# A diffusion transformer block on one core: V's order, the place of the half-head PV, the pieces of the last chunk, and the issue of the K weights

## The chip, the cores and the metric

The kernel runs on one core of a Trainium2 chip. The metric is device time in microseconds; lower is better.

Names: PE is TensorE's matmul, PEld its weight load, DVE VectorE, ACT ScalarE, POOL GpSimd, SP SyncE. "L688" is line 688 of that kernel's source; the change adds lines, so L1284 of the kernel before is L1289 of the changed one. "Half-head PV": a head has 576 columns, four times 128 plus 64; the two halves of 64 of both heads share one 128-row tile and are multiplied side by side in column tiles of 64.

## The reference

```python
B, N, D = 2, 256, 1152; F = 4 * D; H = 2; Dh = 576
mod = (silu(c) @ w_mod).reshape(B, 6, 1, D)     # shift_a, scale_a, gate_a, shift_m, scale_m, gate_m
h = layernorm(x) * (1 + scale_a) + shift_a
q, k, v = split(h @ wqkv)
a = softmax(q k^T * Dh**-0.5) v @ wo
x = x + gate_a * a
h2 = layernorm(x) * (1 + scale_m) + shift_m
return x + gate_m * (gelu(h2 @ w_fc1) @ w_fc2)
```

Everything is bfloat16 outside, with sums in float32.

## The kernel before

A scheduler inside the kernel fixes each engine's order at build time: PE and SP in program order, the others by a list scheduler with cost constants. The parts that matter here, with cuts (`...`):

```python
# start: loads on SP, in this order
for b in range(2):
    dma(X[:, 2 * b:2 * b + 2, :], xv[b], ..., "ld_x%d" % b)
for (ka, kb) in ((0, KC), (KC, KT)):
    for k0, k1 in ((0, 3), (3, 6), (6, 9)):
        dma(WSC[:, k0:k1, ka * P:kb * P], wmod_v[...], ..., "ld_sc%d_%d" % (ka, k0))   # scale weights
    for kt in range(ka, kb):
        dma(WK[:, kt, :], wqkv_v[:, kt, D:2 * D], ..., "ld_wk%d" % kt)                 # K weights
...
# middle: V pieces between softmaxes and transposes, then the modulation rows
v_proj(2, 0)
rows()            # gate rows: products in column tiles of 32, stored to DRAM, read back broadcast (GA)
...
v_proj(2, 1); v_proj(2, 2); v_proj(3, 0); rows_T(); v_proj(3, 1); v_proj(3, 2)
...
pv_halves()       # half-head PV: column tiles of 64, and its two evictions
for b in range(2):
    for h in range(2):
        pv(b, h)
wo_tile(0); wo_tile(1); wo_tile(2, ...)   # product with wo, times GA, plus x, layer norm
xn2_T(0)                                  # PE transposes the normalised tile 0
...
# end: the last token tile of fc2 in five pieces: 384, 384, 224, 96, 64 columns
```

## Time and profile before

| | kernel before |
|---|---|
| time, first three runs | 243.79, 243.87, 244.35 us |
| span of the profiled run | 242.3 us |
| PE busy | 238.4 us (98%) |
| first K product starts | 11.18 us |
| last data for the last store ready | 240.79 us |

How to read it: PE is busy all the time, so the end of the span is the sum of PE's own spacings, whatever starts PE's first dense work, and the tail after the last matmul. A line of a time line has start, duration, engine, source line, operation, shapes, count, and in brackets the engine's idle time before it with what ended it. The lines themselves stand in the prediction. One more is needed later, from the page's table of DMA queues (packets, MB, share of the engines):

```profile
q8 instruction: 14, 0.23, 0.4%
```

### The profile page before, as it was taken

To read this page: it belongs to the slowest core of one execution; us is meant where nothing else is said; L and a number is where in the kernel's file an instruction comes from. 1 tells how busy PE (TensorE), PEld (TensorE's weight loads), DVE (VectorE), ACT (ScalarE), POOL (GpSimd) and SP (SyncE) were. 2 spreads that over 40 slices of the span, in tenths; PEclk is the share of its full clock that TensorE was granted. 3 is DMA by queue.
4 is the path that set the end of the run, shared out by engine and by line. 5 is a ranking of instruction groups with operands and counts; after the bars stand their busy time and mean duration, and the time that the engine had idled before them with its cause. 6 is when DMAs were issued, how large, how long until landed. Compare 5 with 4: busy or idle time off the path is not lost.

```text
span 242.3 us, 4076 instructions
## 1 busy us (share of the span) xinstructions
PE 238.4 (98%) x1763; PEld 147.5 (61%) x1763; DVE 120.3 (50%) x218; ACT 67.0 (28%) x136; POOL 21.2 (9%) x39
## 2 busy tenths in 40 slices
PE   7999999999999999999999999999999999999996
PEld 2698854556667666898444444444566656656676
DVE  3814388696997699789999500000022222111112
ACT  5820350355424107973233322222000000000000
POOL 1400000000021186400000000020000000000000
PEclk9999999999999999999999999999999999999999
DMA  6999999999996999989953498012000000000001
GB/s 241 330 381 392 391 392 391 397 413 405 391 356 196 351 395 391 391 266 394 314 164 82 150 320 313 0 29 72 0 16 19 16 16 19 16 16 16 19 24 27
DMA packets 30140, 51.59 MB, mean 213 GB/s; under 512 B 1703, under 2 KB 15787, under 8 KB 30123
## 3 DMA queue, kind: packets, MB, share of 16 engines
q1 hardware_dynamic: 29680, 50.14, 58.0%
q0 software_dynamic: 416, 1.19, 1.6%
q8 instruction: 14, 0.23, 0.4%
q14 instruction: 3, 0.02, 0.0%
q10 hardware_dynamic: 27, 0.00, 0.0%
HBM read 50.14 MB, written 1.19 MB: 212 GB/s over the span
## 4 chain that ended last, share of the span: by engine, by line
PE 97%; DVE 2%; POOL 0%; issue 0%; ACT 0%; DVEq 0%; POOLq 0%
PE psum L688 95%; PE psum L691 2%; DVE arena L739 1%; DVE arena L760 0%; POOL arena L711 0%; DVE arena L740 0%; DVE arena L1284 0%; DVE arena L1285 0%; POOL arena L710 0%; ACT arena L726 0%; DVE arena L727 0%; DVE arena L732 0%; DVE arena L742 0%; POOL arena L717 0%; POOL arena L715 0%
## 5 line engine op out<-in xcount | busy, mean ns | idle before, releaser
L688 PE MATMUL psum<-arena 128*128 128x384 bf16 (+10 forms) x1674 | 234.9, 306 | 1.6 <-POOL arena L711 1.5
L688 PEld LDWEIGHTS psum<-arena 128*128 128x128 bf16 (+3 forms) x1674 | 142.3, 97 | 90.0 <-issue 3.8
L1079 DVE SCALAR_TENSOR_TENSOR arena<-arena 128x1152 f32<-128x1152 bf16 x32 | 44.7, 1414 | 0.6
L1284 DVE TENSOR_TENSOR arena<-psum,arena 128x384 f32<-128x384 f32 (+3 forms) x14 | 7.0, 501 | 68.0 <-PE psum L688 68.0
L1193 ACT ACTIVATE arena<-psum 128x512 bf16<-128x512 f32 (+1 forms) x44 | 22.4, 520 | 42.7 <-PE psum L688 42.7
L683 ACT ACTIVATE arena<-psum 128x512 bf16<-128x512 f32 (+6 forms) x37 | 19.6, 549 | 39.5 <-PE psum L688 37.1
L685 DVE CAST arena<-psum 128x512 bf16<-128x512 f32 (+3 forms) x13 | 8.2, 641 | 11.4 <-PE psum L688 11.3
L669 POOL DMA_DIRECT2D dit_scratch<-arena x3 | 1.8, 616 | 115.7 <-DVE arena L685 58.9
L1161 POOL TENSOR_TENSOR arena<-arena 128x384 f32<-128x384 f32 x12 | 10.9, 910 | 10.8 <-DVE arena L1160 9.5
L1106 DVE CAST arena<-psum 72x32 bf16<-72x32 f32 x1 | 0.2, 186 | 21.3 <-PE psum L688 21.3
L739 DVE BATCH_NORM_STATS2 arena<-arena 128x6 f32<-128x384 f32 (+1 forms) x18 | 9.5, 552 | 0.1
L1166 ACT ACTIVATE arena<-arena 128x1152 bf16<-128x1152 f32 x4 | 5.3, 1345 | 11.9 <-DVE arena L1165 11.9
L691 PEld LDWEIGHTS psum<-arena 128*128 128x128 bf16 (+1 forms) x89 | 5.8, 98 | 2.5 <-issue 0.8
L1160 DVE TENSOR_TENSOR arena<-psum,arena 128x384 f32<-128x384 f32 x12 | 6.5, 549 | 1.6 <-DMA arena<-dit_scratch 1.6
L1285 DVE TENSOR_TENSOR arena<-arena 128x384 bf16<-128x384 f32 (+3 forms) x14 | 7.0, 501 | 0.5
L691 PE MATMUL psum<-arena 128*128 128x128 bf16 (+1 forms) x89 | 7.1, 219 | 0.1
L1180 DVE TENSOR_SCALAR arena<-psum,arena 128x128 bf16<-128x128 bf16 x20 | 5.4, 341 | 1.9 <-PE psum L691 1.9
L1183 ACT ACTIVATE arena<-psum,arena 128x128 bf16<-128x128 bf16 x16 | 6.0, 456 | 0.9 <-PE psum L688 0.6
L1086 DVE TENSOR_REDUCE arena<-arena 128x36 f32<-128x1152 f32 x4 | 5.4, 1348 | 0.0
L1083 DVE STREAM_TRANSPOSE arena<-arena 128x1152 f32<-128x1152 f32 x4 | 5.4, 1364 | 0.0
L1009 ACT ACTIVATE arena<-psum,arena 128x256 bf16<-128x256 f32 x8 | 3.7, 472 | 1.3 <-PE psum L688 0.9
L743 POOL TENSOR_TENSOR arena<-arena 128x1 f32<-128x1 f32 x6 | 3.6, 596 | 2.0 <-DVE arena L742 2.0
(48 smaller groups left out, 44.9 us busy)
## 6 DMA issues: line engine op xcount, KB each, us to landing
arena<-in_w_fc_dram SPq DMA_DIRECT2D x9, 1152.0 KB, 7.3
arena<-in_w_fc_dram SPq DMA_DIRECT2D x4, 2592.0 KB, 17.2
arena<-in_wqkv_dram SPq DMA_DIRECT2D x18, 288.0 KB, 10.2
arena<-in_w_mod_dram SPq DMA_DIRECT2D x3, 1728.0 KB, 20.2
arena<-in_w_mod_dram SPq DMA_DIRECT2D x3, 864.0 KB, 13.7
arena<-in_w_mod_dram SPq DMA_DIRECT2D x9, 288.0 KB, 10.5
arena<-in_wqkv_dram SPq DMA_DIRECT2D x1, 2592.0 KB, 16.6
arena<-in_wo_dram SPq DMA_DIRECT2D x1, 2592.0 KB, 24.4
```

What stands on the lines that cost most here:

```text
L683: act(c_act(n), lambda e: e.activation(out=dst, in_=src, func=ACTF.Copy), [src], [dst], name)
L685: dve(c_dve_psum16(n) if psum16 else c_dve_psum32(n), lambda e: e.tensor_copy(dst, src), [src], [dst], name)
L688: S.instr(lambda e: e.matmul(o, lhsT=l, rhs=r, start=st, stop=sp, **kw), reads=[l, r], writes=[o])
L691: S.instr(lambda e: e.transpose(o, i_, idn), reads=[i_, idn], writes=[o])
L739: dve(550, lambda e, s=s, o=o: e.bn_stats(out=o, in_=s), [s], [o], "bn_%s_%d" % (tag, ci))
L1079: dve(1270, lambda e, w=w, s=s, acc=acc: e.scalar_tensor_tensor(out=acc, in0=w, scalar=s, in1=acc, op0=ALU.mult, op1=ALU.add), [w, s, acc] ...
L1160: dve(550, lambda e, o=o, ga=ga, x1c=x1c: e.tensor_tensor(out=x1c, in0=o, in1=ga, op=ALU.mult), [o, ga], [x1c], "wo_t1_%d_%d" % (t, ci))
L1161: S.op("pool", 930, lambda e, xs=xs, x1c=x1c: e.tensor_tensor(out=x1c, in0=x1c, in1=xs, op=ALU.add), reads=[x1c, xs], writes=[x1c], name=" ...
L1183: act(440, lambda e, o=o, dst=dst, s1=s1, s2=s2: e.activation(out=dst, in_=o, func=ACTF.Identity, scale=s1, bias=s2), [o, s1, s2], [dst], ...
L1193: act(c_act(ntok), lambda e: e.activation(out=dst, in_=o, func=ACTF.Gelu_apprx_tanh), [o], [dst], "gelu_%d_%d" % (f, tok0))
L1284: dve(c_dve_psum32(w), lambda e, o=o, gm=gm, t1=t1: e.tensor_tensor(out=t1, in0=o, in1=gm, op=ALU.mult), [o, gm], [t1], "fc2_t1_%d_%d" % ( ...
L1285: dve(c_dve_32(w), lambda e, t1=t1, x1c=x1c, ost=ost: e.tensor_tensor(out=ost, in0=t1, in1=x1c, op=ALU.add), [t1, x1c], [ost], "fc2_out_%d ...
```

## The change

The intent: let the half-head PV stand directly ahead of the modulation rows, so that the array changes its tiling once less. For that V's middle columns, which the half-head PV reads, must be made first. The evictions of the half-head PV stay behind the last V piece, because they overwrite V's input. The last chunk of 320 columns beside the final 64 is no longer cut in two. SP holds the K weights until the second half of x is there.

```diff
-                    if ins is last_out:
+                    if ins is outs[-2]:
                         for o in outs[:-4]:
                             eng_handle.wait_ge(dma_sems[o.dma_sem], o.dma_val)
...
                 dma(WK[:, kt, :], wqkv_v[:, kt, D:2 * D], P * D * 2, "ld_wk%d" % kt, run=2304)
+                if kt == 0:
+                    S.instrs[-1].deps.update(j for j in S.instrs if j.name == "ld_x1")
...
-        v_proj(0, 0)
-        s_and_softmax(0, 1)
         v_proj(0, 1)
+        s_and_softmax(0, 1)
+        v_proj(1, 1)
         s_and_softmax(1, 1)
-        v_proj(0, 2)
+        v_proj(2, 1)
         pt_transposes(0, 0)
...
         v_proj(2, 0)
+        pv_halves()
         rows()
...
         v_proj(3, 2)
+        pv_halves_ev()
...
-        pv_halves()
         for b in range(2):
             for h in range(2):
                 pv(b, h)
...
-  pieces = [(0, CH), (CH, 2 * CH), (2 * CH, 3 * CH - 160), (3 * CH - 160, 3 * CH - 64), (3 * CH - 64, 3 * CH)]
+  pieces = [(0, CH), (CH, 2 * CH), (2 * CH, 3 * CH - 64), (3 * CH - 64, 3 * CH)]
```

More of the change, by code (lines that the diff above doesn't have):

```diff
@@ L1119, in pv_halves, with pv_halves_ev @@
                            kjt == 0, kjt == 1, tile_position=(0, 64 * h))
+        def pv_halves_ev():
             for b, eng in ((0, "dve"), (1, "act")):
@@ L1209, in build_kernel @@
         proj(WQ, 8, 8, HX, 2)
-        v_proj(0, 0)
-        s_and_softmax(0, 1)
-        v_proj(0, 1)
-        s_and_softmax(1, 1)
-        v_proj(0, 2)
-        pt_transposes(0, 0)
+        v_proj(0, 1)
+        s_and_softmax(0, 1)
+        v_proj(1, 1)
+        s_and_softmax(1, 1)
+        v_proj(2, 1)
+        pt_transposes(0, 0)
+        v_proj(3, 1)
+        pt_transposes(1, 0)
+        v_proj(0, 0)
+        pt_transposes(0, 1)
         v_proj(1, 0)
-        pt_transposes(1, 0)
-        v_proj(1, 1)
-        pt_transposes(0, 1)
-        v_proj(1, 2)
         pt_transposes(1, 1)
         v_proj(2, 0)
+        pv_halves()
         rows()
@@ L1225, in build_kernel @@
         wfc1_load(1)
-        v_proj(2, 1)
+        v_proj(3, 0)
+        v_proj(0, 2)
+        v_proj(1, 2)
+        rows_T()
         v_proj(2, 2)
-        v_proj(3, 0)
-        rows_T()
-        v_proj(3, 1)
         v_proj(3, 2)
+        pv_halves_ev()
         wfc1_load(2)
```

## The prediction

> **What bounds the kernel now.** I read the page's busy times and chain first, then the table of waits, then the time line engine by engine, and at last the single records of the trace (start of one matmul to start of the next).
>
> ```profile
> PE 238.4 (98%) x1763; PEld 147.5 (61%) x1763; DVE 120.3 (50%) x218; ACT 67.0 (28%) x136; POOL 21.2 (9%) x39
> PE 97%; DVE 2%; POOL 0%; issue 0%; ACT 0%; DVEq 0%; POOLq 0%
> PE psum L688 <- POOL arena L711: 1.5, 1, 1.5
> ```
>
> The first line is busy time, the second the chain that ended last, the third the whole answer for waits of PE: apart from its first 1.5 us TensorE is never shown idle. A busy PE is not a PE at its peak, so I checked the spacing of starts. From 11 us to the end a 384-column matmul follows another after 162 ns, a 512-column one after 216, a 256-column one after 109, and only 17 places lose more than 12 ns beyond that. So nothing can be gained by taking work off another engine; only fewer or cheaper matmuls, the few lossy places, the first 11 us and the tail are to be had. Those are what the change touches. The lossy places of the middle:
>
> ```profile
> 63.96 1.29 PEld L688 LDWEIGHTS psum<-arena 128*128 128x128 bf16 x9
> 65.57 2.06 PEld L688 LDWEIGHTS psum<-arena 128*2 128x2 bf16 x72 [0.32 <-issue]
> 67.88 7.35 PEld L688 LDWEIGHTS psum<-arena 128*128 128x128 bf16 x55 [0.25 <-issue]
> 75.55 0.36 PEld L688 LDWEIGHTS psum<-arena 128*64 128x64 bf16 x8 [0.32 <-issue]
> 76.10 0.99 PEld L688 LDWEIGHTS psum<-arena 128*128 128x128 bf16 x10 [0.20 <-issue]
> ```
>
> This is the time line of the weight loads. The 72 narrow loads are the modulation rows (column tiles of 32), the 8 loads at 75.55 the half-head PV (column tiles of 64); before and after each the loads pause. In the single records the gaps at these four borders are 94, 96, 94 and 96 ns longer than the matmul itself. The tail:
>
> ```profile
> 234.10 0.56 DVE L1284 TENSOR_TENSOR arena<-psum,arena 128x384 f32<-128x384 f32 x1 [4.70 <-PE psum L688]
> 237.55 0.39 DVE L1284 TENSOR_TENSOR arena<-psum,arena 128x224 f32<-128x224 f32 x1 [2.30 <-PE psum L688]
> 239.08 0.26 DVE L1284 TENSOR_TENSOR arena<-psum,arena 128x96 f32<-128x96 f32 x1 [0.71 <-PE psum L688]
> 240.31 0.22 DVE L1284 TENSOR_TENSOR arena<-psum,arena 128x64 f32<-128x64 f32 x1 [0.68 <-PE psum L688]
> 240.57 0.22 DVE L1285 TENSOR_TENSOR arena<-arena 128x64 bf16<-128x64 f32 x1
> ```
>
> Each L1284 starts when a piece of the last product is complete, so its 36 matmuls took 3.45 us at 224 columns, 1.53 at 96, 1.23 at 64; the piece of 384 columns ahead took 5.85. VectorE waits for PE every time. The start:
>
> ```profile
> 3.37 2.50 SPq L669 DMA_DIRECT2D arena<-in_wqkv_dram  x4
> 9.11 0.41 PEld L688 LDWEIGHTS psum<-arena 128*128 128x128 bf16 x13 [0.23 <-DMA arena<-in_w_mod_dram]
> 10.32 0.38 PEld L688 LDWEIGHTS psum<-arena 128*128 128x128 bf16 x12 [0.17 <-DMA arena<-in_w_mod_dram]
> 11.18 1.91 PE L688 MATMUL psum<-arena 128*128 128x256 bf16 x16
> ```
>
> The four first K weights are issued from 3.37 us. PE waits twice for the scale weights; they were issued from 1.69 to 2.69 us and take 6.3 to 7.6 us to land. The first K product starts at 11.18: K weight 0 lands 7.7 us after its issue, at 11.07, while the activations it needs are written by VectorE at 10.96. So that product starts on a DMA, by 0.1 us.
>
> **What the Trainium skill says.** "TensorEngine Tiling (Array Packing)", section Key Properties: changing the tiling mode, not only the tile, drains TensorE. The trace agrees, with 94 to 96 ns at each of the four borders. "TensorE: Matmul & The Clock Gate", section Back-to-back issue gap: isolated matmuls follow each other after N/2.4 + 2.5 ns. Here 5.85/36 = 162.5, 3.45/36 = 95.8 and 1.53/36 = 42.5 ns, the formula to 0.1 ns. The same page, section The cost: per-tile semaphore tail: semaphore increments of matmuls serialize, its fit giving 26.3 ns each. The 64-column piece agrees in kind: its matmuls start every 29.1 ns, yet 1.23/36 = 34.2 ns is what each costs VectorE, the increments being recorded 34 ns apart. "DMA: Bandwidth & Descriptors", section Queues, rings and completion order: on each DMA engine the descriptors of one issuing engine are consumed in ring order. The landings agree: x, scale weights, K weights, in issue order.
>
> **The last chunk in two pieces.** Removed: 36 matmuls and their loads. The columns are the same 320, so only the fixed part goes: 36 x (320/2.4 + 2.5) = 4.89 us against 3.45 + 1.53 = 4.98. Saved on PE: 0.09 us, all on the path. What could eat it is VectorE: 320 columns, between 0.39 us at 224 and 0.56 at 384, make 0.49 for each of two operations, 1.02 with the gaps. The 64-column piece still takes 1.23, so VectorE is free 0.2 us before it is wanted. One output less is stored; its issue (0.33 us on SyncE) is beside the path. The waits for old outputs, which go before the last but one store instead of the last, ran on SyncE in the records from 240.04 to 240.37 us, while the last data were ready at 240.79. They are hidden now. Left where they were they would come 0.33 us after the store of the 320 columns is issued (1.42 us after that piece) and end at about 1.80, against last data at 1.74; so the move keeps some 0.05 us from being lost and gains nothing over the kernel before. Sum: -0.09.
>
> **Half-head PV ahead of the rows.** The twelve V pieces are the same matmuls in another order, and softmaxes and transposes stay where they stood between them: 0. Half-head PV next to the rows makes three borders of tiling mode of four: -0.095. If the passage from 64 to 32 columns costs less than the others, up to -0.19; I take one. The PV needs the last transposed probabilities: transposed at 63.79, copied by about 65.0, wanted at 65.57. No wait. Its evictions must still follow the last V piece, since they overwrite the V product's input; they find both engines free there.
>
> The price: the rows come later. Half-head PV takes 0.35 us between first and last start, plus 0.205 to the next, so rows and their eviction move from 68.32 to 68.88. From there a chain runs to PE:
>
> ```profile
> 68.32 0.46 DVE L685 CAST arena<-psum 98x288 bf16<-98x288 f32 x1
> 80.42 1.34 DVE L1086 TENSOR_REDUCE arena<-arena 128x36 f32<-128x1152 f32 x1
> 83.32 0.56 DVE L1160 TENSOR_TENSOR arena<-psum,arena 128x384 f32<-128x384 f32 x1 [1.56 <-DMA arena<-dit_scratch]
> 83.80 1.34 DVE L1086 TENSOR_REDUCE arena<-arena 128x36 f32<-128x1152 f32 x1
> 91.02 1.35 ACT L1166 ACTIVATE arena<-arena 128x1152 bf16<-128x1152 f32 x1 [10.61 <-DVE arena L1165]
> 92.95 0.67 PE L691 MATMUL psum<-arena 128*128 128x128 bf16 x9
> ```
>
> The rows are stored, read back as gates (VectorE waits for that until 83.32), and then VectorE, GpSimd and ScalarE work without a pause until the normalised tile 0 is there at 92.37. PE transposes it at 92.95: slack 0.58, less some 0.03 for the semaphore. The chain moves by +0.56, PE arrives 0.095 earlier: the demand is 0.655 against 0.55, a stall of 0.1 us. The gates' landing (7.3 us after issue, beside weight loads that fill the DMA engines) may well move by half a microsecond either way. A stall is cut off at zero, so I expect 0.15 on average: +0.15. Later transposes have over a microsecond to spare, and the accumulators of the output projection too.
>
> **K weights held back.** SyncE would issue them from x of batch 1's landing, 1.22 + 4.6 = 5.8 us, instead of 3.37. The three scale loads ahead of them are under way until 10.3 us. The first K packet ran at about 8.7, and an issue needs some 1.2 us to become packets: 7.1, still in time. x itself landed at full speed (its second half 1.45 us after the first), so there is nothing to free it from. I expect 0, with a small hope that the scale weights, whose last engine lags the others by 0.3 to 0.6 us, come sooner: -0.03.
>
> **Sum:** -0.09 - 0.095 + 0.15 - 0.03 = -0.065. From 243.87 that is 243.8; since one of the three runs before was 0.5 above the others, I put the median a little lower, 243.75.
>
> **The rivals.** *The gate chain takes over*: if the rows' eviction slips behind one more row sum (1.35 us each on VectorE; four ran just before it and ended at 68.27), the gates come over a microsecond late and the stall is about 0.9 us: 244.5. Against: the shift is under half of such an operation. One chance in eight. *The start gains*: were K traffic what delays the scale weights, their two waits (0.23 and 0.17) and the K weight's 0.1 could go, until VectorE binds: -0.35, so 243.35. Against: ring order and landings. One in six. *The start loses*: the ring runs dry, K weights land later and every following product too: +0.3, 244.1. One in eight. *All slack holds*: no stall, so 243.6 to 243.65. One in three.
>
> **Range and chances.** The fixed savings are 0.19 us; the start and the stall spread about that by some -0.35 to +0.7, and the runs by 0.1 to 0.2. So 243.2 to 244.3. A change of 2% is 4.9 us, far beyond all of it: within 2% 0.985, faster 0.008, slower 0.007.
>
> **What would show it.** In the profile after: 36 matmuls fewer, L1284 of 128x320 near 0.49 us, 4.9 us after the piece before and 1.23 before the last; three pauses of the weight loads around 65 to 68.5 us and none at 75; rows evicted near 68.9; a wait of PE or its loads of 0 to 0.3 us for ScalarE near 92.9; SyncE's K issues from 5.8 and the first K product still at 11.1 to 11.3. A first K product moved by over 0.2, a row eviction after 69.3, or any PE wait over 0.3 us elsewhere would make the prediction wrong.

## The result

The changed kernel took 243.83 us (median of 6 runs, 243.76 to 244.34), the kernel before 244.09 in its 6 runs (243.79 to 244.5). The ratio is 0.9995, with a 95% interval of 0.998 to 1.0009: the same within 2%, and not told apart from 1. The ratios here and below are the record's own, made from the fast runs of the same rounds, so they are not quite the ratios of the medians quoted.

Where both kernels ran again beside the experiments, the same picture came back. All 28 runs of the kernel before have a mean of 244.22 us (standard deviation 0.31), all 11 of the changed one 243.99 (0.21). The difference of 0.2 us is no larger than what one run differs from the next, so the times alone are a poor guide to a cause. The single records of the trace are a better one, because they repeat to a few nanoseconds.

The spans of the runs, which the record lists too, say more than the times. Where the changed kernel ran again, its spans were 242.26 us on average (5 runs) and those of the kernel before in the same rounds 242.83 (9 runs): 0.57 us shorter, which is clear of the scatter. But the time beside the span was 1.75 us instead of 1.35. Over all runs with a recorded span it was 1.69 to 1.80 in the changed kernel (11 runs) and 1.25 to 1.43 in the kernel before (22 runs). So some 0.40 us of what was gained inside the span was lost after it. The traces show a part of where. After the span's end only one transfer runs, a packet of 8 KB of a queue that is marked "instruction" as well (q14). It started 0.60 and 0.62 us after the end of the span in the two profiles of the kernel before, 1.07 and 1.04 us after it in those of the changed kernel. The experiments tell which edit brings this.

The profiled run of the changed kernel happened to be one of its longer ones (244.31 us, span 242.6), and its span is 0.21 us *longer* than that of the kernel before. Its parts show why. The weight loads, over the same stretch as in the prediction:

```profile
64.44 1.29 PEld L688 LDWEIGHTS psum<-arena 128*128 128x128 bf16 x9
66.04 0.36 PEld L688 LDWEIGHTS psum<-arena 128*64 128x64 bf16 x8 [0.32 <-issue]
66.60 2.06 PEld L688 LDWEIGHTS psum<-arena 128*2 128x2 bf16 x72 [0.20 <-issue]
68.91 8.12 PEld L688 LDWEIGHTS psum<-arena 128*128 128x128 bf16 x61 [0.25 <-issue]
```

Three pauses instead of four; in the single records they cost 92, 93 and 97 ns. The passage from tiles of 64 to tiles of 32 costs as much as the others. The tail, DVE's time line:

```profile
234.47 0.56 DVE L1289 TENSOR_TENSOR arena<-psum,arena 128x384 f32<-128x384 f32 x1 [4.70 <-PE psum L688]
...
239.36 0.49 DVE L1289 TENSOR_TENSOR arena<-psum,arena 128x320 f32<-128x320 f32 x1 [3.74 <-PE psum L688]
...
240.59 0.22 DVE L1289 TENSOR_TENSOR arena<-psum,arena 128x64 f32<-128x64 f32 x1 [0.21 <-PE psum L688]
240.85 0.23 DVE L1290 TENSOR_TENSOR arena<-arena 128x64 bf16<-128x64 f32 x1
```

The piece of 320 columns took 239.36 - 234.47 = 4.89 us, and DVE still waits 0.21 us for the last one. The start, SP's issue and PE's first K product:

```profile
5.97 1.76 SPq L669 DMA_DIRECT2D arena<-in_wqkv_dram  x4
...
9.07 0.98 PEld L688 LDWEIGHTS psum<-arena 128*128 128x128 bf16 x26
...
10.69 0.46 PE L688 MATMUL psum<-arena 128*128 128x2 bf16 x12
...
11.55 2.01 PE L688 MATMUL psum<-arena 128*128 128x256 bf16 x16
```

The K weights go out at 5.97 instead of 3.37, and the first K product starts at 11.55 instead of 11.18. Whether the first causes the second is the main question for the experiments. And the gate chain, from the rows' eviction to the transposes of the normalised tile 0:

```profile
69.35 0.46 DVE L685 CAST arena<-psum 98x288 bf16<-98x288 f32 x1 [0.61 <-PE psum L688]
...
83.10 0.56 DVE L1164 TENSOR_TENSOR arena<-psum,arena 128x384 f32<-128x384 f32 x1 [0.97 <-PE psum L688]
...
90.79 1.35 ACT L1170 ACTIVATE arena<-arena 128x1152 bf16<-128x1152 f32 x1 [10.02 <-DVE arena L1169]
...
93.32 0.67 PE L691 MATMUL psum<-arena 128*128 128x128 bf16 x9
```

Rows are evicted 1.03 us later than before, yet the product with the gates (L1164) starts 0.22 us *earlier*, and the tile is normalised 1.2 us before PE transposes it, not 0.58.

Cutting the span at four PE events makes the comparison exact. "First transposes" are those of the probabilities (58.73 us in the kernel before), "tile transposes" those of the normalised tile 0. The columns: landing of K weight 0 (its last engine), start of the first K product, from there to the first transposes, from those to the tile transposes, from those to the start of the last matmul, and the rest of the span.

| profile | K weight 0 landed | first K product | to first transposes | to tile transposes | to last matmul | rest |
|---|---|---|---|---|---|---|
| before | 11.05 | 11.18 | 47.55 | 34.215 | 146.951 | 2.445 |
| before, again | 11.86 | 12.00 | 47.55 | 34.215 | 146.951 | 2.598 |
| changed | 11.42 | 11.56 | 47.65 | 34.109 | 146.861 | 2.372 |
| changed, again | 11.21 | 11.35 | 47.55 | 34.108 | 146.861 | 2.379 |
| changed, no hold | 11.49 | 11.62 | 47.55 | 34.109 | 146.861 | 2.378 |
| before + hold | 11.69 | 11.83 | 47.55 | 34.215 | 146.951 | 2.545 |
| before + two pieces | 11.36 | 11.49 | 47.55 | 34.215 | 146.862 | 2.371 |
| before + PV first | 11.58 | 11.72 | 47.55 | 34.109 | 146.951 | 2.382 |
| changed, PV split | 10.94 | 11.07 | 47.64 | 34.336 | 146.862 | 2.370 |
| changed, waits last | 11.54 | 11.68 | 47.55 | 34.108 | 146.861 | 2.434 |

From the first row to the third: +0.37 at the start, +0.10 up to the first transposes, -0.106, -0.090, -0.073: together the +0.21 by which that span is longer. The +0.10 are two waits of PE shortly after the first K product: 0.04 us for ScalarE's copy of the activations and 0.06 for K weight 1, which landed 0.97 us after K weight 0 in this profile and 0.70 to 0.84 us after it in the other profiles with whole K weights.

### The profile page after: what moved, and what is told of

It reads as the page before. It is cut to its first block, busy times and chain, and to the rows that moved or that the text cites. A ratio compares the mean times of both kernels' runs of the same rounds, so it can differ in the third digit from the quotient of the medians.

```text
span 242.6 us, 3989 instructions
## 1 busy us (share of the span) xinstructions
PE 238.3 (98%) x1717; PEld 146.4 (60%) x1727; DVE 120.0 (49%) x216; ACT 66.9 (28%) x136; POOL 21.7 (9%) x39
## 4 chain that ended last, share of the span: by engine, by line
PE 98%; issue 0%; POOL 0%; DVE 0%; POOLq 0%
PE psum L688 96%; PE psum L691 2%; POOL arena L713 0%; DVE arena L1289 0%; DVE arena L1290 0%; POOL arena L712 0%; POOL arena L719 0%; POOL arena L717 0%; POOLq L1351 0%
## 5 line engine op out<-in xcount | busy, mean ns | idle before, releaser
L688 PE MATMUL psum<-arena 128*128 128x384 bf16 (+9 forms) x1628 | 235.0, 310 | 2.0 <-POOL arena L713 1.5
L688 PEld LDWEIGHTS psum<-arena 128*128 128x128 bf16 (+1 forms) x1638 | 141.1, 97 | 91.8 <-issue 4.7
L1289 DVE TENSOR_TENSOR arena<-psum,arena 128x384 f32<-128x384 f32 (+2 forms) x13 | 6.9, 527 | 68.3 <-PE psum L688 68.3
L1170 ACT ACTIVATE arena<-arena 128x1152 bf16<-128x1152 f32 x4 | 5.3, 1343 | 11.3 <-DVE arena L1169 11.3
L1164 DVE TENSOR_TENSOR arena<-psum,arena 128x384 f32<-128x384 f32 x12 | 6.5, 550 | 1.3 <-PE psum L688 1.2
L691 PEld LDWEIGHTS psum<-arena 128*128 128x128 bf16 (+1 forms) x89 | 5.9, 98 | 2.1 <-DMA arena<-in_c_dram 0.8
L1290 DVE TENSOR_TENSOR arena<-arena 128x384 bf16<-128x384 f32 (+2 forms) x13 | 6.9, 527 | 0.4
## 6 DMA issues: line engine op xcount, KB each, us to landing
arena<-in_w_mod_dram SPq DMA_DIRECT2D x9, 288.0 KB, 11.1
```

The lines of the kernel that those rows point to most:

```text
L688: S.instr(lambda e: e.matmul(o, lhsT=l, rhs=r, start=st, stop=sp, **kw), reads=[l, r], writes=[o])
L691: S.instr(lambda e: e.transpose(o, i_, idn), reads=[i_, idn], writes=[o])
L1164: dve(550, lambda e, o=o, ga=ga, x1c=x1c: e.tensor_tensor(out=x1c, in0=o, in1=ga, op=ALU.mult), [o, ga], [x1c], "wo_t1_%d_%d" % (t, ci))
L1289: dve(c_dve_psum32(w), lambda e, o=o, gm=gm, t1=t1: e.tensor_tensor(out=t1, in0=o, in1=gm, op=ALU.mult), [o, gm], [t1], "fc2_t1_%d_%d" % ( ...
L1290: dve(c_dve_32(w), lambda e, t1=t1, x1c=x1c, ost=ost: e.tensor_tensor(out=ost, in0=t1, in1=x1c, op=ALU.add), [t1, x1c], [ost], "fc2_out_%d ...
```

## The experiments

Each kernel was one edit away from the kernel before or from the changed one. The theory: the middle and the tail save what the table shows, the start differs from run to run in every kernel, and (to be tested) the hold makes it later. The rival: the hold is neutral. "Beside the span" is a run's time less its span; the kernel before had a mean span of 242.91 us and 1.33 us beside it in the rounds of the first four experiments.

### The changed kernel without the hold

```diff
                 dma(WK[:, kt, :], wqkv_v[:, kt, D:2 * D], P * D * 2, "ld_wk%d" % kt, run=2304)
-                if kt == 0:
-                    S.instrs[-1].deps.update(j for j in S.instrs if j.name == "ld_x1")
```

> The changed kernel without the hold on the K weights. Theory 1 (the middle and the tail save 0.2 to 0.27 us, the hold costs 0.1 to 0.3 by making the first K weights land later, and the moment at which the PE clock is released adds 0 to 0.6 us at random to any run of any kernel): K weight 0 lands near 11.0 us again, not 11.4; the fastest runs are 0.2 to 0.3 us below the fastest of the kernel before. Rival (the hold is neutral, the later landing in the changed kernel's profile was that run's own): it equals the changed kernel, fastest runs within 0.07 us of 243.76.

Measured: median 244.27 us of 6 runs (243.87 to 244.53), ratio to the kernel before of the same rounds 0.9997 (0.9983 to 1.0012). K weight 0 landed at 11.49, not near 11.0. The theory's number failed: in this profile the landing stayed late although the hold was gone. In the times neither side was right: the fastest run was 0.12 us above the fastest of the kernel before (243.75), where the theory wanted it 0.2 to 0.3 below and the rival within 0.07 of 243.76. The spans were 242.45 us on average, with 1.75 beside them.

### The kernel before plus the hold alone

```diff
                 dma(WK[:, kt, :], wqkv_v[:, kt, D:2 * D], P * D * 2, "ld_wk%d" % kt, run=2304)
+                if kt == 0:
+                    S.instrs[-1].deps.update(j for j in S.instrs if j.name == "ld_x1")
```

> The kernel before plus the hold alone. Theory 1: the first K products start 0.1 to 0.4 us later relative to the last scale weights' landing, fastest runs 0.1 to 0.3 us above those of the kernel before. Rival (neutral): fastest runs within 0.07 us of it, K weight 0 landing at 11.0 to 11.1 us.

Measured: median 244.02 us of 6 runs (243.69 to 244.47), ratio 0.9991 (0.9976 to 1.0006). Its fastest run, 243.69, is within 0.07 of the fastest of the kernel before (243.75), as the rival said. Its profile had K weight 0 at 11.69, 0.98 us behind the last scale weights, which still spoke for a cost; so the two signs pointed in opposite directions, and more profiles were needed. The spans were 242.73 us on average, with 1.32 beside them.

### The kernel before plus the two pieces alone

```diff
-                    if ins is last_out:
+                    if ins is outs[-2]:
...
-  pieces = [..., (2 * CH, 3 * CH - 160), (3 * CH - 160, 3 * CH - 64), (3 * CH - 64, 3 * CH)]
+  pieces = [..., (2 * CH, 3 * CH - 64), (3 * CH - 64, 3 * CH)]
```

> The kernel before plus the last chunk in two pieces alone. Both theories: last chunk on PE 4.89 + 1.02 us instead of 4.98 + 1.02; fastest runs 0.09 to 0.16 us below the kernel before (0.09 on PE, up to 0.07 in the last store). If the tail hides it: within 0.04.

Measured: median 244.26 us of 6 runs (243.88 to 244.65), ratio 1.0 (0.9983 to 1.0017). In the times nothing shows: the fastest run is 0.13 us above that of the kernel before, not 0.09 to 0.16 below. In the records the stretch to the last matmul is 146.862 instead of 146.951, the 0.09 us expected, and the rest 2.371. The spans of its runs say why the times hide it: they were 242.53 us on average, 0.38 shorter, but 1.73 us lay beside them instead of 1.33. So this edit alone brings the loss after the span, and not by the moved waits, since the kernel that left them ahead of the last store has it too (1.77). All kernels with two pieces have it (1.68 to 1.80) but one, the kernel with half of K weight 0 first (1.22 to 1.29); no kernel with three pieces has it (1.20 to 1.43). In those with the loss the last 8 KB packet starts 1.04 to 1.29 us after the end of the span, in the others 0.45 to 0.62. What the exception has beside its half weight is one more load on SP, so that SP issues as many transfers as in the kernel before. That this decides is a guess from the count; no run isolates it, and the cause stays open.

A second difference lies in the rest itself. In the four profiles with three pieces that rest was 2.38 to 2.60, in the seven with two pieces and the waits moved 2.37 to 2.38. In all four with three pieces one 16 KB packet of queue q8, which the page calls "instruction", starts 0.26 to 0.52 us before the start of the last matmul and takes 0.88 to 1.32 us; the first small store, 448 bytes a row, lands on its last engine 1.5 to 1.9 us after the start of the last matmul in three of them, though its other engines were done by 0.01. That the packet held up this engine fits in time but is inferred, since the records do not say on which engine a packet ran. In the two-piece kernel this packet is missing altogether:

```profile
q8 instruction: 13, 0.21, 0.4%
```

That the 72 instructions fewer on PE are why it is missing is plausible from the count, but no run isolates it.

### The kernel before plus V's order and the half-head PV ahead of the rows

The edit is the part of the diff above that moves `v_proj`, `pv_halves` and `pv_halves_ev`, and nothing else.

> The kernel before plus the V order and the half-head PV ahead of the rows alone. Theory 1: one border of tiling mode fewer, PE 0.10 us earlier at the first transposes of the normalised tile and no wait there, because the rows' store lands with the weight loads it queues among, not a fixed time after its issue; fastest runs 0.1 us below the kernel before. Rival of the prediction (gates late by 0.56 us): a gap of 0.1 to 0.5 us at that transpose, and no gain or a loss.

Measured: median 243.93 us of 6 runs (243.8 to 244.7), ratio 0.9991 (0.9975 to 1.0007). The stretch to the tile transposes is 34.109 instead of 34.215, and PE does not wait there. Theory and records agree to 0.01 us; the rival from the prediction, gates that come late, is out. In the times the fastest run, 243.80, is not 0.1 us below that of the kernel before (243.75), as was expected; the spans were 242.73 us on average, 0.18 shorter, with 1.30 beside them.

### The changed kernel again

No edit.

> The changed kernel once more, for a second profile and more times. All profiles so far start the first K product 0.13 us after K weight 0 has landed, and from there to the half-head PV no kernel differs. Theory 1 (held K weights land later behind the scale weights): K weight 0 lands 0.90 us or more after the last scale weights of the first half, as in both held profiles so far (0.94, 0.98), against 0.75 to 0.77 in the four unheld ones; middle segment (first transposes of the probabilities to those of the normalised tile) 34.11 us, from there to the last matmul 146.86. Rival: the interval scatters over both ranges.

Measured: median 244.0 us of 5 runs (243.84 to 244.19), ratio 0.9995 (0.9982 to 1.0007). K weight 0 landed at 11.21, 0.74 us behind the last scale weights, as in the unheld kernels. So the theory that held weights lag behind fell. Over all profiles with four whole first K weights and the hold as in the change, it landed at 11.42, 11.69, 11.21, 10.94 and 11.54 (mean 11.36); without it at 11.05, 11.49, 11.36, 11.58 and 11.86 (mean 11.47). The lag behind the scale weights was 0.74 to 0.98 with the hold, 0.75 to 0.87 without. No effect of the hold is seen in ten profiles; with landings that scatter by 0.3 us (standard deviation) they cannot exclude some tenths of a microsecond either way. The spans hint at a small gain rather than a loss (with the hold alone 242.73 against 242.91), which is not clear of the scatter.

What is common to all ten is that the first K product starts 0.135 us after the landing of K weight 0. That landing varies by 0.9 us from run to run, while what follows it varies far less, so it is the main noise of the profiled spans. The moment at which the PE clock is released is not: it lay anywhere from 4.7 to 7.8 us in the profiles that record it. In the two with the latest release (7.71 and 7.76) the first transposes of x came latest (8.59 and 8.62 us, against 7.97 to 8.34 in the others), but PE then still waited for K weight 0.

### Half of K weight 0 first

```diff
-                dma(WK[:, kt, :], wqkv_v[:, kt, D:2 * D], ..., "ld_wk%d" % kt, run=2304)
-                if kt == 0:
-                    S.instrs[-1].deps.update(j for j in S.instrs if j.name == "ld_x1")
+                if kt == 0:
+                    for h0, h1 in ((0, 512), (512, D)):
+                        dma(WK[:, 0, h0:h1], wqkv_v[:, 0, D + h0:D + h1], ..., "ld_wk0_%d" % h0)
+                else:
+                    dma(WK[:, kt, :], wqkv_v[:, kt, D:2 * D], ..., "ld_wk%d" % kt, run=2304)
```

> The changed kernel without the hold, K weight 0 loaded in two pieces (512 columns first), so that the first K products wait for half of it. Theory 1 (the first K product is bound by the landing of K weight 0): it starts 0.15 to 0.35 us after the last scale weights' landing less than before, bound then by the scaled activations; fastest runs 0.2 to 0.45 us below the fastest of the kernel before, the best of all. Rival (the time before the first K product is taken back at K weight 1): the first K product moves, the broadcast shift rows do not, and the time stays that of the unheld kernel.

Measured: median 243.83 us of 5 runs (243.66 to 244.12), ratio 0.999 (0.9977 to 1.0004): not told apart from 1. The first half landed at 10.95, but the first K product started only at 11.39, bound now by the scaled activations, 0.82 us after the last scale weights instead of 0.88 to 0.90 where whole weights were in time. The 0.08 us was given back four products later: to the first transposes it took 47.63 us instead of 47.55. So the rival was right that the time is taken back, but not where. PE waited there for ScalarE's copy of the activations (done at 11.76), and not at K weight 1, which was in time. The runs have the lowest mean of the set, 243.85 us, and the spans say why: at 242.60 us on average they are no shorter than those of the other kernels with two pieces, but only 1.25 us lies beside them. This is the exception named above, and the fastest kernel here for a reason that the edit was not made for.

### A longer hold

```diff
-                    S.instrs[-1].deps.update(j for j in S.instrs if j.name == "ld_x1")
+                    S.instrs[-1].deps.update(j for j in S.instrs if j.name == "ld_sc0_6")
```

> The changed kernel with the hold made longer: K weights are issued only when the last scale weights of the first half have landed (about 10.5 us). Theory 1: K weight 0 lands some 2 us after that, near 12.6, the first K product at 12.8, 1.2 us later than in the changed kernel, and the whole kernel 1.1 to 1.6 us longer; the x and scale weights land as ever, 4.3 to 4.8 and 10.3 to 10.8, so holding traffic back frees nothing. Rival (the hold relieves the earlier loads): scale weights land 0.3 us or more earlier than in any other profile.

Measured: 247.24 and 247.46 us, ratio 1.0132 (1.0112 to 1.0151). K weight 0 landed at 12.83 and the first K product started 0.135 us later, as the theory says; the scale weights landed at 10.14, within 0.05 us of the earliest of the other profiles (10.19), so holding traffic back frees nothing. But the cost is 3.35 us over the changed kernel in the same rounds (244.0), more than twice the expectation. SP's and PE's time lines, and the table by stretch (PE, PEld, DVE, ACT and POOL busy with counts, granted clock, DMA share, GB/s):

```profile
10.16 1.77 SPq L669 DMA_DIRECT2D arena<-in_wqkv_dram  x4
```

```profile
12.97 3.52 PE L688 MATMUL psum<-arena 128*128 128x256 bf16 x16 [1.73 <-DMA arena<-in_wqkv_dram]
```

```profile
13.00:16.00 3.00, 3.00 (x15) 2.08 (x16) 0.00 (x0) 0.00 (x0) 0.00 (x0) 0.50 0.93 281
```

After PE's pause of 1.73 us the granted clock is 0.50 for 3.4 us (12.89 to 16.30 in the clock records), and the 256-column products follow each other after 213 ns, not 109. The first K product was 1.6 us later than in the changed kernel's second profile, and the stretch to the first transposes 49.16 us, 1.6 longer: together the 3.24 us by which the span is longer. This is what a hold costs once it is too long.

### The half-head PV cut in two

```diff
-        pv_halves()
+        pv_halves((0,))
+        v_proj(3, 0)
+        pv_halves((1,))
         rows()
...
-        v_proj(3, 0)
```

> The changed kernel with the half-head PV cut into batch 0 and batch 1, one V piece between them: two more borders of tiling mode, and the rows 1.5 us later. Theory 1 (each border costs 0.095 us of PE time): middle segment 34.11 + 0.19 = 34.30 us, with or without the few ns of the cut; no wait at the transposes of the normalised tile as long as the rows' store lands with the weight loads. Rival (half of the saving was something else, such as the waits of the half-head PV): under 0.1 us.

Measured: 244.01 us in one look. The weight loads:

```profile
65.55 0.14 PEld L688 LDWEIGHTS psum<-arena 128*64 128x64 bf16 x4 [0.32 <-issue]
65.88 1.25 PEld L688 LDWEIGHTS psum<-arena 128*128 128x128 bf16 x9 [0.20 <-issue]
67.45 0.14 PEld L688 LDWEIGHTS psum<-arena 128*64 128x64 bf16 x4 [0.32 <-issue]
67.79 2.06 PEld L688 LDWEIGHTS psum<-arena 128*2 128x2 bf16 x72 [0.20 <-issue]
```

Two borders more cost 0.227 us (34.336 against 34.109): 94 and 96 ns at the two added borders in the single records, and the rest, 0.04 us, at the cut beside them. The saving of the change in the middle is the border, and it can be bought and sold by count.

This kernel also answers why the later rows did no harm. POOL's time line (rows stored, then read back), first in the kernel before, then in the changed one, then in this one:

```profile
69.32 1.25 POOL L669 DMA_DIRECT2D dit_scratch<-arena  x2 [58.92 <-DVE arena L685]
75.97 1.13 POOL L669 DMA_DIRECT2D arena<-dit_scratch  x2 [5.40 <-DMA dit_scratch<-arena]
```

```profile
70.36 1.25 POOL L669 DMA_DIRECT2D dit_scratch<-arena  x2 [59.61 <-DVE arena L685]
76.25 1.13 POOL L669 DMA_DIRECT2D arena<-dit_scratch  x2 [4.64 <-DMA dit_scratch<-arena]
```

```profile
71.57 1.25 POOL L669 DMA_DIRECT2D dit_scratch<-arena  x2 [60.81 <-DVE arena L685]
76.06 1.13 POOL L669 DMA_DIRECT2D arena<-dit_scratch  x2 [3.23 <-DMA dit_scratch<-arena]
```

Counted from the first transposes of each run, the store is issued after 10.59, 11.15 and 12.86 us and has landed after 16.70, 16.50 and 16.80. The later the issue, the shorter the wait: the landing does not depend on the issue in this range. It comes within half a microsecond of the landing of the large fc1 weight load issued ahead of it (16.97, 16.33, 16.46). The read-back then lands after 24.50, 23.80 and 24.02 us; the tile is normalised after 33.63, 32.93 and 32.92; PE transposes it after 34.22, 34.11 and 34.34.

The first profile of the kernel before is the latest of its kind, though. In its second profile the read-back landed after 23.72 us and the tile was normalised after 32.86, as early as in the changed kernel. Over all profiles the tile was normalised after 32.86 to 33.63 us in the old order (four profiles) and after 32.69 to 32.93 in the new one (eight). So the later rows do no harm; that they make the tile come earlier is not shown.

### The waits left ahead of the last store

```diff
-                    if ins is outs[-2]:
+                    if ins is outs[-1]:
```

> The changed kernel with the waits for old outputs left ahead of the last store. The prediction's claim: they run after the store of the 320 columns and end 0 to 0.1 us after the last data are ready, so from the start of the last matmul to the end of the span it is 2.40 to 2.47 us instead of 2.37 to 2.38. Rival: they end before the data are ready and nothing moves (2.37 to 2.38).

Measured: the rest of the span is 2.434 us, 0.06 more than 2.37 to 2.38. In the records the five waits run from 240.80 to 241.12 and the last store is issued at 241.175, while its data were ready at 241.088; with the waits moved it goes out 0.03 us after its data. The prediction's small claim holds. (244.37 us; the time alone would show nothing.)

### The kernel before again

No edit.

> The kernel before once more, for a second profile of it. If run-to-run time is set by the landing of K weight 0: first K product 0.12 to 0.14 us after it, middle segment 34.215, then 146.951 to the last matmul, whatever the run's time; span less that landing 231.2 to 231.4 us, against 231.0 to 231.15 for kernels with both savings. Rival: the segments themselves scatter by a tenth or more.

Measured: 244.61 us in one look. K weight 0 landed at 11.86 and the first K product started 0.135 us later; the two stretches came out at 34.215 and 146.951 again. From the first K product to the end of the span the kernels with four borders and three pieces took 231.16, 231.26 and 231.31 us; the changed kernel took 231.00 in its first profile, which includes the 0.10 us lost after the first K product, and 230.90 in its second. So what the change really saves in the span is 0.2 us in the middle and on the last matmuls, plus 0 to 0.2 in the last stores, in any profile, under a start that moves by up to 0.9 us. After the span it loses 0.40.

## Why the prediction was right

The measured 243.83 us is 0.08 above the predicted 243.75 and inside the range; the change was forecast as next to nothing, and it was. That the number is so close is in part luck. The forecast added to the span a stall of 0.15 us that did not come, and left out the 0.40 us after the span, which did. It also started from 243.87, the median of the first three runs, while all six runs set beside the changed kernel's have 244.09. Two of the signs that the prediction itself had named against it did appear in the first profile: the first K product moved by 0.37 us (named: over 0.2), and the rows were evicted at 69.35 (named: after 69.3). Both come from the start, which had moved as much from one profile of the kernel before to the next. Step by step:

- **Last chunk in two pieces, -0.09:** right inside the span, -0.090 in every kernel that has it. DVE's 0.49 us per operation and its 0.2 us to spare came out as 0.49 and 0.21. Missed: the last stores, which also end 0.01 to 0.23 us sooner with two pieces; and the 0.40 us that this edit alone adds after the span. The prediction looked only at what happens inside it. In time this step gained nothing (244.26 against 244.17 us, medians).
- **The moved waits:** right. They protect 0.06 us (predicted some 0.05) that the two pieces would otherwise have lost, and gain nothing else.
- **One border of tiling mode fewer, -0.095:** right, -0.106, and confirmed from the other side by two more borders, +0.227.
- **Half-head PV early enough, no wait:** right; the loss at its entry is only the border.
- **The rows 0.56 us later, +0.15 by a stall at the tile transposes:** this step was wrong. The rows did come 0.56 us later counted from the first transposes. The failed sentence is "The chain moves by +0.56". The trace already had the clue that the store took 5 us for 2 KB beside full DMA queues, but the prediction treated that as a fixed delay after its issue. In the runs the store's landing does not follow its issue: issued anywhere from 10.6 to 12.9 us after the first transposes, it landed after 16.2 to 16.8 in all twelve profiles. The slack before the tile transposes was 1.18 to 1.42 us in the new order. The 0.58 from which the prediction started was the smallest of four profiles in the old order (0.58 to 1.36), so it had taken one value of a scattered quantity as fixed.
- **The hold on the K weights, 0 with a small hope of -0.03:** right in size, as far as ten profiles can tell. The reason given, that the weights wait in ring order behind the scale weights anyway, fits the longer hold, where only the issue being later than the queue could bear made the landing late. Its numbers were a little off: in the trace that it read the first K packet ran at 8.96 us, not about 8.7, and the load of x became packets 1.0 us after its issue, where the prediction reckons with 1.2.
- **First K product still at 11.1 to 11.3:** missed (11.56 and 11.35), but that need not come from the change: the kernel before itself had 11.18 and 12.00. What the prediction had seen rightly is that this product starts on a DMA; that this landing is what makes runs differ was only to be seen with more profiles.
- **Net:** inside the span the forecast of -0.065 was too small by the stall that did not come, +0.15, and by the last stores. From the first K product to the end of the span the saving is 0.2 to 0.4 us. The 0.40 us after the span takes it back, and what is left in the times is smaller than their scatter.

## What to carry to other kernels

Where an engine is busy all the time, cut its trace at a few of its own events and compare the stretches: 0.1 us that a handful of timed runs does not show repeats there to a few nanoseconds, and a scattered start is seen as what it is. Compare the time beside the span too: here it differed by 0.40 us between kernels, more than anything that the change gained at one place. Put products in narrow tiles next to each other, even where their widths differ, since every border costs the same here. Before moving a transfer's issue, ask what its landing follows: a small store among full queues and a load behind other loads both landed when the queue let them, and only a hold that emptied the queue cost anything, and then it cost the PE clock too.

## What the Trainium skill lacked or had wrong

- "TensorEngine Tiling (Array Packing)", Key Properties, says that a change of tiling mode drains TensorE and gives no size. Here each border cost 92 to 97 ns, and the one from column tiles of 64 to column tiles of 32 cost 93, no less than those to and from the whole array.
- "TensorE: Matmul & The Clock Gate", The cost: per-tile semaphore tail, gives 26.3 ns for each increment, for packed tiles. Here a plain stream of 64-column matmuls started every 29 ns but was recorded on its semaphore every 34 ns, so that 36 of them cost their reader 1.23 us.
- The same page, Part 1, gives ±500 ns for the moment at which the clock is released and about 3.4 us of idle for its loss. Here release lay between 4.7 and 7.8 us in the profiles that record it, and a pause of 1.73 us, behind a microsecond of matmuls with 2 and 128 columns, was followed by half the clock for 3.4 us.
- "DMA: Bandwidth & Descriptors", Queues, rings and completion order, says that engines take the queues in turn by packet. It has no figure for a small store from GpSimd beside a full SyncE queue; here 2 KB took 3 to 6 us and landed within 0.5 us of the weight load issued ahead of it, whether it was issued 10.6 or 12.9 us after the reference point.
- "Runtime: NRT & Kernel Launch", Instruction fetch mechanics, tells of instruction refills in blocks of 16 KiB and calls what a boundary costs mostly hidden; it has no time for a block, and nothing on the end of a run. Here 13 or 14 packets of 16 KB ran on the "instruction" queue in each profile and took 0.88 to 1.59 us each. After the end of the span an 8 KB packet started 0.45 to 0.62 us later in some kernels and 1.04 to 1.29 in others, and the time beside the span differed by 0.40 us between these groups.
